# A retention, top-capacity experts and an ELU layer in one kernel: six dense pieces beside the retention, a fetch timed behind its scatters, one ELU step on VectorE

## The chip, the cores and the metric

The kernel runs on one core of a Trainium2 chip. The metric is the device time of one execution in microseconds. The kernel before takes 535.06 us in the median of three runs (534.75 to 536.52). The execution that was profiled took 536.38 us.

## What is computed

Three layers follow each other. All inputs are float32.

```python
# 1: retention over B=2, H=8, S=768, D=64, in blocks of 64, with a state per head
intra = (qb @ kb.T * Dmask) @ vb ; inter = (qb * lam_pow) @ kv_state
out[block] = intra + inter
kv_state = lam_block * kv_state + (kb * rev_pow).T @ vb
# 2: x is [1536, 512]; eight experts, each takes at most 192 tokens
logits = x @ w_gate                       # [1536, 8]
for idx in argsort(-logits.flatten()):    # best pair (token, expert) first
    if token is free and counts[expert] < 192: assign
out[mask_e] = relu(x[mask_e] @ w1[e]) @ w2[e]     # 512 -> 1024 -> 512
# 3: a dense layer over all tokens
h = x @ w_in                              # 512 -> 2048
g = where(h > 0, h, exp(min(h, 0)) - 1)
result = g @ w_out                        # 2048 -> 512
```

The greedy assignment fills one expert after another: the expert whose 192nd token has the highest threshold is closed first, its tokens leave, and the rest is counted again.

## The kernel before

**Retention.** Twelve tiles of 128 tokens (n = 0 to 11) pass through transposes (L292), scores (L316), a masked product (L320 on VectorE), outputs (L329, L340), gate logits (L383, L410) and a state update (L365 on VectorE, L354 on GpSimd). Each tile's best logits are turned into rows (L455, L458) and compared with the others on VectorE (L435, L439, L442, L467). TensorE counts the results in 8-column matmuls (L447), from which a first rank comes.

**The dense pieces.** w_in and w_out arrive as 64-bit numbers in 16 pieces of 1 MB (L224, into the two buffers stg). Each piece is split by five steps: L252, L255 and L258 on VectorE make a float32 f, L260 on ScalarE its float16 high part (wih or woh), and L261 on VectorE the low part (wil or wol). Five pieces are split beside the retention, and the loads of two more are issued there. The other pieces are split beside the experts.

**The experts.** For k = 0 to 7 a choice is made: a threshold (L831, L832, L840), the chosen tokens (L883 to L885), and index counts, 1-column matmuls of `mt` with the shifted one-hot `ohs` (L898), one per tile and per column of `idx`. L904 copies each column. GpSimd then gathers the chosen rows of x from memory (xb at L917, xa at L923). TensorE transposes them (L964), L973 or L976 and L981 copy them as xt, and then come the groups h = x w1 (L1076, or L1043 to L1045 in float16), y = h w2 (L1116, or L1043 to L1045), g = y w_in (L1043 to L1045) and, after each second expert, o = g w_out (L1211 to L1213). h and y pass through ScalarE and VectorE on their way (L1087, L1091, L1126, L1130). The ELU of g (`g_evac`) has three steps on ScalarE (L1183 to L1185), then the maximum on VectorE (L1186), and a split in two float16 halves (L1191, L1192). Outputs leave through ot (L1224) and an indirect store by GpSimd (L1231).

**Updates and packing.** After choice k, `update` takes the remaining tokens' best logits (L763), turns them into rows (transposes L781, copies L784), compares them (L435, L439, L442) and counts (L804). For the choices after k = 1, 3 and 5 the open tokens are first packed: each tile's records are scattered by GpSimd to a packed list in memory (L731) and the list is fetched again (L744, L748). From the third on, each scatter waits for the last TensorE instruction that the program has issued before it.

**What sets the order.** A class `Plan` takes tasks with an engine, a cost, the tasks each depends on, a `lag` after its end and a bonus `ahead`, and places them in time. The order of its `at` times is the order of the instructions on every engine. One plan covers the retention (with the dense pieces beside it), a second one everything from the first threshold on. The numbers there are the author's, not the trace's.

Of the kernel before, what the change touches and what calls it, by code (L numbers as in the profile page):

```python
# [24 lines left out]
OP = mybir.AluOpType  # L25
# [16 lines left out]
LATE = 11  # L42

# [59 lines left out]
def kernel(  # L103
# [82 lines left out]
    def lam_in():  # L186
        nc.scalar.dma_start(lamb, bass.AP(tensor=lam.tensor, offset=lam.offset, ap=[[0, 128], [1, H]]))
# [300 lines left out]
    put("lam", "ACT", 0.5, lam_in, lag=2.8, ahead=100.0)  # L488
    put("dec", "DVE", 2.7, decays, T["eye"], T["lam"], ahead=190.0)
    put("gate", "ACT", 1.9, gate_in, lag=3.0, ahead=90.0)  # L490
    put("qsc", "DVE", 1.6, q_scales, T["lam"], T["dec"], ahead=20.0)
# [10 lines left out]
    for n in range(NT):  # L502
        c = n % NC

        soon = PITCH * (NT - 1 - n) - BEHIND
        if n + 1 < NT:
            fed(n + 1)
# [7 lines left out]
        if c:  # L515
            put(("qS", n), "POOL", 1.3, lambda n=n: q_scaled(n), *of(("qTo", n), ("inter", n - 2), ("inter", n - 3), "qsc"))
# [18 lines left out]
        put(("scored", n), "PE", 0.88, lambda n=n: scored(n), *of("gate", ("xT0", n), ("xT1", n), ("L", n - 2)), mode="A", ahead=soon)  # L535
        put(("L", n), "ACT", 0.18, lambda n=n: logits(n), *of(("scored", n)), ahead=soon)
        put(("m", n), "DVE", 0.18, lambda n=n: top_logit(n), *of(("L", n)), ahead=soon)
        put(("row", n), "PE", 0.22, lambda n=n: row(n), *of(("m", n), ("rowo", n - 1)), mode="A", ahead=soon)
        put(("rowo", n), "ACT", 0.29, lambda n=n: row_out(n), *of(("row", n)), ahead=soon)
# [41 lines left out]
    use, use2 = [None, None], [None, None]  # L581
    for i in range(EARLY_N + NEXT):
        ld = add("SP", 2.9, lambda i=i: load_dense(i), T["ld", "v", 1], use[i % 2])
        if i < EARLY_N:
# [10 lines left out]
            use2[i % 2] = add("DVE", 1.19, lambda go=go: go(4), d)  # L595
# [97 lines left out]
    def pack(k):  # L693
# [45 lines left out]
        for c in range(n):  # L739
# [5 lines left out]
                    p, lag=4.0, ahead=AHEAD)  # L745
# [569 lines left out]
```

## Time and profile before

| | |
|---|---|
| median of three runs | 535.06 us (534.75 to 536.52) |
| the profiled execution | 536.38 us, its span 534.3 us |
| instructions in the span | 12976 |
| TensorE (PE) busy | 507.6 us, 95% of the span |
| VectorE (DVE), ScalarE (ACT), GpSimd (POOL) busy | 360.8, 306.5, 92.9 us |
| mean granted TensorE clock | 0.976 |
| moved by DMA | 70.42 MB, mean 132 GB/s |

The times are microseconds from the start of the span. A matmul's row shows its whole passage, so in a run of matmuls the distance of two starts is what each costs the engine. A DVE or ACT row is an instruction, or, with xN, N of the same kind. What stands in brackets is how long the engine had been idle before that instruction and what released it. In the windows the granted clock is a share of 2.4 GHz.

### The profile page before, as it was taken

What the parts mean: (1) busy time and instruction counts of PE and PEld (TensorE: products, weight loads), DVE (VectorE), ACT (ScalarE), POOL (GpSimd) and SP (SyncE); (2) the same over time, 40 slices, a digit from 0 to 9 for tenths busy, and PEclk for the clock granted to TensorE, in tenths of its full rate; (3) what the DMA queues carried; (4) which work ended last, traced back from release to release, by engine and by line L of the source; (5) the groups of instructions that cost most, each with busy time, mean ns of one, the idle gap of its engine ahead of it and who ended that gap; (6) DMA issues with size and microseconds to landing.
All of it is one profiled execution on the core that took longest, in us unless ns stands there. A gap on an engine that the chain in (4) does not pass through costs nothing.

```text
span 534.3 us, 12976 instructions
## 1 busy us (share of the span) xinstructions
PE 507.6 (95%) x5362; PEld 426.5 (80%) x5362; DVE 360.8 (68%) x808; ACT 306.5 (57%) x646; POOL 92.9 (17%) x124
## 2 busy tenths in 40 slices
PE   8999886899999899999999999999999999999994
PEld 7887776799899874589869956996997489879941
DVE  6689998987999697486587675637557552671510
ACT  5777744324883665445982784468449533961910
POOL 3231420200345002030441101012401001000000
PEclk9999996799999999999999999999999999999997
DMA  9999934394686104240440324052205504040000
GB/s 208 219 285 236 292 127 140 106 372 184 209 299 197 50 1 176 85 144 11 182 162 25 128 80 162 18 190 89 95 3 188 178 21 188 1 178 1 2 21 20
DMA packets 62218, 70.42 MB, mean 132 GB/s; under 512 B 40160, under 2 KB 44720, under 8 KB 61136
## 3 DMA queue, kind: packets, MB, share of 16 engines
q1 hardware_dynamic: 57456, 62.66, 36.6%
q0 software_dynamic: 2960, 6.66, 3.7%
q8 instruction: 42, 0.69, 0.5%
q10 hardware_dynamic: 1744, 0.28, 0.3%
q14 instruction: 16, 0.13, 0.1%
HBM read 63.08 MB, written 6.51 MB: 130 GB/s over the span
## 4 chain that ended last, share of the span: by engine, by line
PE 68%; DVE 15%; issue 6%; DMA 5%; ACT 4%; POOL 1%; POOLq 0%; ACTq 0%; DVEq 0%
PE ps_t L1043 5%; PE ps_t L1044 5%; PE ps_s L1044 5%; PE ps_s L1043 5%; PE ps_s L1045 5%; PE ps_t L1045 5%; PE ps_s L1213 3%; PE ps_s L1211 3%; PE ps_s L1212 3%; PE ps_S L1043 2%; PE ps_S L1044 2%; PE ps_S L1045 2%; PE ps_s L1076 2%; PE ps_t L1211 2%; PE ps_t L1212 2%
## 5 line engine op out<-in xcount | busy, mean ns | idle before, releaser
L1044 PE MATMUL ps_t<-yt,wih 128*128 128x192 f16 x208 | 51.2, 246 | 0.8 <-DVE yt L1130 0.8
L1045 PE MATMUL ps_t<-yt,wil 128*128 128x192 f16 x208 | 51.2, 246 | 0.0
L1043 PE MATMUL ps_t<-yt,wih 128*128 128x192 f16 x208 | 51.1, 246 | 0.0
L1045 PEld LDWEIGHTS <-wil 128*128 128x128 f16 x512 | 50.1, 98 | 1.0 <-issue 0.9
L1043 PEld LDWEIGHTS <-wih 128*128 128x128 f16 x512 | 50.3, 98 | 0.0
L1044 PEld LDWEIGHTS <-wih 128*128 128x128 f16 x512 | 50.0, 98 | 0.2
L1045 PE MATMUL ps_s<-yt,wil 128*128 128x192 f16 x200 | 49.2, 246 | 0.0
L1044 PE MATMUL ps_s<-yt,wih 128*128 128x192 f16 x200 | 49.2, 246 | 0.0
L1043 PE MATMUL ps_s<-yt,wih 128*128 128x192 f16 x200 | 49.2, 246 | 0.0
L731 POOL DMA_INDIRECT open<-rec,dest x27 | 31.3, 1159 | 49.7 <-DVE dest L720 18.3
L1213 PEld LDWEIGHTS <-gg 128*128 128x128 f16 x192 | 18.8, 98 | 23.4 <-DVE gg L1192 0.9
L1213 PE MATMUL ps_s<-woh,gg 128*128 128x512 f16 x96 | 36.4, 379 | 0.4 <-DVE gg L1192 0.4
L1212 PE MATMUL ps_s<-wol,gg 128*128 128x512 f16 x96 | 36.4, 379 | 0.0
L1211 PE MATMUL ps_s<-woh,gg 128*128 128x512 f16 x96 | 36.4, 379 | 0.0
L1192 DVE TENSOR_TENSOR gg<-el,gg 128x384 f16<-128x384 f32 x64 | 34.2, 552 | 1.7 <-ACT gg L1191 1.6
L1035 DVE SCALAR_TENSOR_TENSOR w2p<-stg,w2p 128x1024 f16<-128x1024 f32 x24 | 28.3, 1221 | 10.1 <-ACT w2p L1032 10.1
L1184 ACT ACTIVATE el<-el 128x384 f32<-128x384 f32 x64 | 33.4, 522 | 1.9
L1185 ACT ACTIVATE el<-el 128x384 f32<-128x384 f32 x64 | 33.4, 521 | 1.8
L1212 PEld LDWEIGHTS <-gg 128*128 128x128 f16 x192 | 18.8, 98 | 19.4
L1211 PEld LDWEIGHTS <-gg 128*128 128x128 f16 x192 | 18.8, 98 | 19.2
L1191 ACT ACTIVATE gg<-el 128x384 f16<-128x384 f32 x64 | 31.2, 508 | 2.3 <-DVE el L1186 2.3
L923 POOL DMA_INDIRECT xa<-xd,idx x8 | 9.4, 1175 | 132.4 <-DVE idx L904 131.8
(269 smaller groups left out, 1580.7 us busy)
## 6 DMA issues: line engine op xcount, KB each, us to landing
stg<-in_moe_w_dram SPq DMA_DIRECT2D x24, 1024.0 KB, 5.3
stg<-in_moe_w_in_dram SPq DMA_DIRECT2D x7, 1024.0 KB, 7.2
stg<-in_moe_w_out_dram SPq DMA_DIRECT2D x6, 1024.0 KB, 5.7
w1p<-in_moe_w_dram SPq DMA_DIRECT2D x8, 512.0 KB, 4.3
w2p<-in_moe_w_dram SPq DMA_DIRECT2D x8, 512.0 KB, 8.3
kn<-in_k_dram SPq DMA_DIRECT2D x12, 256.0 KB, 5.5
vn<-in_v_dram SPq DMA_DIRECT2D x12, 256.0 KB, 5.6
xd<-xN SPq DMA_DIRECT2D x12, 256.0 KB, 4.0
```

Source lines behind the costliest of these rows:

```text
L731: st = nc.gpsimd.indirect_dma_start(out=buf, out_offset=bass.IndirectOffsetOnAxis(ap=dest[:, c:c + 1], axis=0), in_=rec[:, c, :], in_offse ...
L1035: nc.vector.scalar_tensor_tensor(part(1), T["t"][:, 1024 * z:1024 * z + 1024], sc, part(0), op0=OP.mult, op1=OP.subtract)
L1043: nc.tensor.matmul(o, wh, xh, start=first, stop=False, skip_group_check=True)
L1044: nc.tensor.matmul(o, wh, xl, start=False, stop=False, skip_group_check=True)
L1045: nc.tensor.matmul(o, wl, xh, start=False, stop=last, skip_group_check=True)
L1184: a = add("ACT", 0.49, lambda: nc.scalar.activation(e_, e_, AF.Exp, scale=-1.0), a, ahead=EAHEAD)
L1185: a = add("ACT", 0.49, lambda: nc.scalar.activation(e_, e_, AF.Copy, scale=SG, bias=-SG), a, ahead=EAHEAD)
L1191: a = add("ACT", 0.49, lambda: nc.scalar.activation(gh, two(e_), AF.Copy), a, *free, ahead=EAHEAD)
L1192: a = add("DVE", 0.53, lambda: nc.vector.tensor_tensor(gl, two(e_), gh, op=OP.subtract), a, ahead=EAHEAD)
L1211: nc.tensor.matmul(p, GH[:, f, c], woh[:, f, :], start=f == 0, stop=False, skip_group_check=True)
L1212: nc.tensor.matmul(p, GH[:, f, c], wol[:, f, :], start=False, stop=False, skip_group_check=True)
L1213: nc.tensor.matmul(p, GL[:, f, c], woh[:, f, :], start=False, stop=f == RF2 - 1, skip_group_check=True)
```

## The change

Ten edits, some of them of numbers that only move the plan.

- `lam` is loaded by GpSimd's queue rather than ScalarE's, and `qsc` is entered later in the plan.
- Six dense pieces rather than five are planned beside the retention. The low step (L261) of the last two of these, pieces 4 and 5, is left to the second plan.
- `HOLD` names a number that was a default, 0.15, and stays at it.
- The fetch of packed tokens is planned 4.3 us behind the last scatter (`(p, 4.3)`), with a lag of its own of 3.0 rather than 4.0.
- On odd k the index counts make two columns rather than three, xb is gathered with 128 rows rather than 64, and the transposed tile is read 64 columns further on (`z0`).
- For k = 0 the second half of the transposed tokens goes to a bank of the ring `work` rather than of `rbank`, where the row transposes take theirs.
- From the third expert on (k = 2 to 7) the third ELU step is a VectorE tensor_scalar rather than a ScalarE copy.

```diff
-EARLY_N, NEXT = 5, 2
-
-LD, PITCH, BEHIND = (1.3, 1.1), 5.5, 2.0
+EARLY_N, NEXT = 6, 2
+
+LEFT_N = 2
+
+LD, PITCH, BEHIND, HOLD = (1.3, 1.1), 5.5, 2.0, 0.15
 AHEAD, XAHEAD, WAHEAD, EAHEAD, GLAG, APART = 15.0, 4.0, 5.0, 3.0, 3.5, 1.2
...
 LATE = 11
+
+LESS_ACT = (2, 3, 4, 5, 6, 7)
...
     def lam_in():
-        nc.scalar.dma_start(lamb, bass.AP(tensor=lam.tensor, offset=lam.offset, ap=[[0, 128], [1, H]]))
+        nc.gpsimd.dma_start(lamb, bass.AP(tensor=lam.tensor, offset=lam.offset, ap=[[0, 128], [1, H]]))
...
     put("orders", "DVE", 0.7, orders, T["eye"], ahead=195.0)
-    put("lam", "ACT", 0.5, lam_in, lag=2.8, ahead=100.0)
+    put("lam", "POOL", 1.0, lam_in, lag=2.8, ahead=100.0)
     put("dec", "DVE", 2.7, decays, T["eye"], T["lam"], ahead=190.0)
     put("gate", "ACT", 1.9, gate_in, lag=3.0, ahead=90.0)
-    put("qsc", "DVE", 1.6, q_scales, T["lam"], T["dec"], ahead=20.0)
...
         if c:
+            if n == 1:
+                put("qsc", "DVE", 1.6, q_scales, T["lam"], T["dec"], ahead=20.0)
             put(("qS", n), "POOL", 1.3, lambda n=n: q_scaled(n), *of(("qTo", n), ("inter", n - 2), ("inter", n - 3), "qsc"))
...
-    use, use2 = [None, None], [None, None]
+    use, use2, left = [None, None], [None, None], []
     for i in range(EARLY_N + NEXT):
...
             d = add("ACT", 1.02, lambda go=go: go(3), d)
-            use2[i % 2] = add("DVE", 1.19, lambda go=go: go(4), d)
+            if i < EARLY_N - LEFT_N:
+                use2[i % 2] = add("DVE", 1.19, lambda go=go: go(4), d)
+            else:
+                left.append((i, go))
     done = hp.order()
...
         fetch = add("POOL", 0.92, lambda: nc.gpsimd.dma_start(new, buf[0:left, :].rearrange("(c p) e -> p c e", p=128)),
-                    p, lag=4.0, ahead=AHEAD)
+                    (p, 4.3), lag=3.0, ahead=AHEAD)
...
-        js = ((0, 128), (64, 0, -64))[k % 2]
+        js = ((0, 128), (64, -64))[k % 2]
+        half = slice(0, 128 if k % 2 else 64)
...
         p = None
-        for j in (1, 0, 2)[0:len(js)]:
+        for j in (1, 0):
             p = add("PE", 0.027 * n, lambda j=j: index(j), (d, 0.3), p, *fills, *(old if j == 1 else ()), ahead=AHEAD)
...
                 nc.vector.tensor_copy(ixm[0:64, k // 2:k // 2 + 1], idx[0:64, k - 1, 1:2])
-                nc.vector.tensor_copy(ixm[64:128, k // 2:k // 2 + 1], idx[64:128, k, 2:3])
-            add("DVE", 0.3, middle, got[2])
+                nc.vector.tensor_copy(ixm[64:128, k // 2:k // 2 + 1], idx[64:128, k, 1:2])
+            add("DVE", 0.3, middle, got[1])
         gb = add("POOL", 1.05, lambda: nc.gpsimd.indirect_dma_start(
-            out=xb[0:64], out_offset=None, in_=xd, in_offset=bass.IndirectOffsetOnAxis(ap=idx[0:64, k, 1:2], axis=0)),
+            out=xb[half], out_offset=None, in_=xd, in_offset=bass.IndirectOffsetOnAxis(ap=idx[half, k, 1:2], axis=0)),
             got[1], *xa_free[0], lag=GLAG, ahead=2 * AHEAD)
...
     def x_parts(k, gb, ga):
-        ca, cb = ((0, 128), (64, 0))[k % 2]
+        ca, cb = ((0, 128), (128, 0))[k % 2]
+        z0 = 64 * (k % 2)
         whole = k in WHOLE
...
             if k == 0:
-                i, old, use = (xbank, rbank)[g].take()
-                tag = ("x", RB_[i])[g]
+                i, old, use = (xbank, work)[g].take()
+                tag = ("x", WB[i])[g]
             else:
...
             def hi(S=S, sl=sl, g=g):
-                pv = S["p"][:, 0:2 * CAP].rearrange("p (a n) -> p a n", a=2)
+                pv = S["p"][:, z0:z0 + 2 * CAP].rearrange("p (a n) -> p a n", a=2)
                 if whole:
...
                 def lo(S=S, sl=sl):
-                    pv = S["p"][:, 0:2 * CAP].rearrange("p (a n) -> p a n", a=2)
+                    pv = S["p"][:, z0:z0 + 2 * CAP].rearrange("p (a n) -> p a n", a=2)
                     nc.vector.scalar_tensor_tensor(xt[:, 1, sl, :], pv, SX, xt[:, 0, sl, :], op0=OP.mult, op1=OP.subtract)
...
         a = add("ACT", 0.49, lambda: nc.scalar.activation(e_, e_, AF.Exp, scale=-1.0), a, ahead=EAHEAD)
-        a = add("ACT", 0.49, lambda: nc.scalar.activation(e_, e_, AF.Copy, scale=SG, bias=-SG), a, ahead=EAHEAD)
+        if k in LESS_ACT:
+            a = add("DVE", 0.3, lambda: nc.vector.tensor_scalar(e_, e_, SG, -SG, op0=OP.mult, op1=OP.add), a, ahead=EAHEAD)
+        else:
+            a = add("ACT", 0.49, lambda: nc.scalar.activation(e_, e_, AF.Copy, scale=SG, bias=-SG), a, ahead=EAHEAD)
         a = add("DVE", 0.53, lambda: nc.vector.tensor_tensor(e_, e_, pv(), op=OP.max), a, ahead=EAHEAD)
...
     R.task = None
+    for i, go in left:
+        dense_done[i] = add("DVE", 1.19, lambda go=go: go(4))
+        f64.uses[i % 2].append(dense_done[i])
     for i in range(EARLY_N, EARLY_N + NEXT):
...
     S_use = work.uses[2]
...
```

TensorE between the first gather and the first expert, before (the tile names: m the best logits, xb and xa the gathered rows, w1p the first weights):

```order
L781 MATMUL ps_o<-identf,m 128x128 x4
L935 MATMUL ps_t_1474<-onesf 128x128 x8
L964 MATMUL ps_x<-identf,xb 128x128 x2
L964 MATMUL ps_m<-identf,xb 128x128 x2
L964 MATMUL ps_x<-identf,xa 128x128 x2
L964 MATMUL ps_m<-identf,xa 128x128 x2
L781 MATMUL ps_m<-identf,m 128x128 x4
L1076 MATMUL ps_s_1615<-xt,w1p 128x192 x8
```

And with the change (gt are the comparisons that L813 counts, L804 before):

```order
L945 MATMUL ps_t_1478<-onesf 128x128 x2
L790 MATMUL ps_o<-identf,m 128x128 x4
L945 MATMUL ps_t_1478<-onesf 128x128
L790 MATMUL ps_m<-identf,m 128x128 x4
L945 MATMUL ps_t_1478<-onesf 128x128 x13
L975 MATMUL ps_x<-identf,xb 128x128 x2
L975 MATMUL ps_s_1608<-identf,xb 128x128 x2
L813 LDWEIGHTS gt_1451
L813 MATMUL ps_o<-oh,gt_1451 128x8
```

The third set of row transposes (L781, now L790) stood behind the gathered rows and stands ahead of them; 12 counting matmuls follow xb, then come xa's transposes, 24 more counts and the first h.

TensorE where the packed tokens of the second packing are turned into rows, before (yt times wih and wil is g of the second expert):

```order
L1045 LDWEIGHTS wil
L1045 MATMUL ps_s_2452<-yt_1444,wil 128x192
L781 MATMUL ps_m<-identf,m 128x128 x4
L781 MATMUL ps_o<-identf,m 128x128 x4
L1043 LDWEIGHTS wih
L1043 MATMUL ps_S<-yt_1444,wih 128x192
L1044 LDWEIGHTS wih
L1044 MATMUL ps_S<-yt_1444,wih 128x192
```

And with the change:

```order
L1056 LDWEIGHTS wil
L1056 MATMUL ps_s_2396<-yt_1448,wil 128x192
L790 MATMUL ps_o<-identf,m 128x128 x4
L790 MATMUL ps_m<-identf,m 128x128 x4
L1054 LDWEIGHTS wih
L1054 MATMUL ps_t_2378<-yt_1448,wih 128x192
L1055 LDWEIGHTS wih
L1055 MATMUL ps_t_2378<-yt_1448,wih 128x192
```

The rows stood behind 72 matmuls of g after the end of y and stand behind 24. The last scatter ahead of them waited for the middle of y's second half and waits now for the last matmul of h.

VectorE at the second half of y of the first expert, before (f_100 and f_99 are pieces being split, idx the index columns, yt the split of y):

```order
L885 TENSOR_TENSOR mt<-me,tid 128x12
L258 SCALAR_TENSOR_TENSOR f_100<-gg,f_100 128x1024
L261 SCALAR_TENSOR_TENSOR wil<-f_99,wih 128x1024
L887 TENSOR_TENSOR act<-act,me 128x12
L700 CAST a_124<-act 128x12
L701 SCALAR_TENSOR_TENSOR a_124<-ones_83,a_124 128x11
L252 TENSOR_SCALAR f_99<-gg 128x1024
L712 COPY rec<-L 128x12x8
L713 CAST rec<-tid 128x12
L255 SCALAR_TENSOR_TENSOR f_99<-gg,f_99 128x1024
L904 CAST idx<-ps_m 128x1 x2
L1130 SCALAR_TENSOR_TENSOR yt_1443<-ps_s_1864,yt_1443 128x384
```

And with the change:

```order
L262 SCALAR_TENSOR_TENSOR f_100<-stg_98,f_100 128x1024
L896 TENSOR_TENSOR act<-act,me 128x12
L709 CAST a_124<-act 128x12
L710 SCALAR_TENSOR_TENSOR a_124<-ones_83,a_124 128x11
L721 COPY rec<-L 128x12x8
L722 CAST rec<-tid 128x12
L727 TENSOR_TENSOR to<-ps_m,after 128x12
L728 TENSOR_TENSOR to<-to,act 128x12
L729 TENSOR_TENSOR dest<-to,after 128x12
L1141 SCALAR_TENSOR_TENSOR yt_1447<-ps_s_1841,yt_1447 128x384
L914 CAST idx<-ps_o 128x1 x2
L1141 SCALAR_TENSOR_TENSOR yt_1447<-ps_t_1883,yt_1447 128x384
```

Of the dense steps ahead of this yt, L261, L252 and L255 have gone behind it. A step L262 (L258 before) of another piece, with its L259 just ahead of the rows shown, stands before the packing's first instructions.

## Rows read from the trace of the kernel before

**Rows 1.** The page, chain that ended last: shares by engine

```profile
PE 68%; DVE 15%; issue 6%; DMA 5%; ACT 4%; POOL 1%; POOLq 0%; ACTq 0%; DVEq 0%
```

**Rows 2.** Windows: PE, PEld, DVE, ACT, POOL busy; clock, DMA share, GB/s

```profile
15.00:30.00 15.00, 14.26 (x208) 11.86 (x208) 11.12 (x19) 11.78 (x40) 4.81 (x5) 1.00 1.01 207
60.00:75.00 15.00, 13.07 (x187) 11.12 (x183) 14.79 (x27) 8.81 (x27) 6.08 (x4) 1.00 0.48 130
75.00:90.00 15.00, 12.20 (x210) 10.69 (x204) 12.97 (x23) 5.40 (x12) 0.00 (x0) 0.73 0.62 211
```

**Rows 3.** PE's waits from 107 us on: us, times, longest

```profile
PE ps_m L781 <- DVE m L763: 2.0, 1, 2.0
PE ps_t L1044 <- DVE yt L1130: 0.8, 1, 0.8
PE ps_m L898 <- ACT ohs L859: 0.4, 1, 0.4
PE ps_s L1213 <- DVE gg L1192: 0.4, 1, 0.4
PE ps_s L1044 <- DVE ht L1091: 0.4, 1, 0.4
```

**Rows 4.** Timeline, 102 to 107 us: start, us, engine, line [idle before]

```profile
103.91 1.22 DVE L261 SCALAR_TENSOR_TENSOR wil<-f,wih 128x1024 f16<-128x1024 f32 x1
104.17 0.44 PE L964 MATMUL ps_x<-identf,xa 128*128 128x128 f32 x2 [1.06 <-DMA xa<-xd,idx]
105.65 1.11 PE L781 MATMUL ps_m<-identf,m 128*128 128x128 f32 x4 [0.82 <-DVE xt L973]
106.56 0.85 PE L1076 MATMUL ps_s<-xt,w1p 128*128 128x192 f32 x2
```

**Rows 5.** Timeline, 133 to 138 us: index counts beside a dense step

```profile
136.03 1.22 DVE L255 SCALAR_TENSOR_TENSOR f<-gg,f 128x1024 uint32<-128x1024 uint32 x1
136.21 0.83 PE L898 MATMUL ps_m<-mt,ohs 128*128 128x1 f16 x27 [0.44 <-ACT ohs L859]
```

**Rows 6.** Timeline, 160 to 182 us: second packing, fetch, row transposes

```profile
162.97 5.36 PE L1116 MATMUL ps_S<-ht,w2p 128*128 128x192 f32 x32
...
171.22 1.34 POOL L731 DMA_INDIRECT open<-rec,dest  x1 [1.35 <-PE ps_t L1116]
177.06 1.06 POOL L744 DMA_DIRECT2D new<-open  x1 [4.50 <-DMA open<-rec,dest]
179.23 0.25 PE L1045 MATMUL ps_s<-yt,wil 128*128 128x192 f16 x1
180.23 0.23 DVE L748 COPY L<-new 128x72 f32<-128x72 f32 x1 [3.71 <-DMA new<-open]
181.47 0.65 PE L781 MATMUL ps_m<-identf,m 128*128 128x128 f32 x4 [2.00 <-DVE m L763]
```

**Rows 7.** Timeline, 226 to 240 us: first and third ot on ACT

```profile
226.35 0.59 ACT L1224 ACTIVATE ot<-ps_S 128x512 f32<-128x512 f32 x1
234.73 0.60 ACT L1224 ACTIVATE ot<-ps_s 128x512 f32<-128x512 f32 x1 [3.87 <-DMA out_dram<-ot,idx]
```

**Rows 8.** Timeline, 0 to 10 us: lam's load and its user

```profile
1.32 0.69 ACTq L187 DMA_DIRECT2D lamb<-in_lam_dram  x1
2.85 0.24 POOL L405 IOTA tid<- 128x12 f16 x1
6.48 2.63 DVE L205 TENSOR_TENSOR_SCAN dec<-lamb,identf 128x128 f32<-128x128 f32 x8 [3.11 <-DMA lamb<-in_lam_dram]
```

**Rows 9.** Timeline, one VectorE step beside a GpSimd step, and alone

```profile
22.85 1.27 POOL L307 TENSOR_TENSOR qS<-qT,qsc 128x512 f32<-128x512 f32 x1 [1.02 <-ACT qT L297]
23.02 1.18 DVE L439 TENSOR_SCALAR w1p<-mrow,m 128x128 f16<-128x128 f32 x1
...
227.81 0.28 DVE L439 TENSOR_SCALAR gt<-mrow,m 128x128 f16<-128x128 f32 x1
```

**Rows 10.** The page, costliest groups: third step of the ELU

```profile
L1185 ACT ACTIVATE el<-el 128x384 f32<-128x384 f32 x64 | 33.4, 521 | 1.8
```

More of the change, by code (lines that the diff above doesn't have):

```diff
@@ L505 @@
         soon = PITCH * (NT - 1 - n) - BEHIND
+        hold = HOLD if n >= NT - 2 else 0.15
         if n + 1 < NT:
@@ L534 @@
                 *of(("intra", n), ("scored", n - 2), ("nat", n - 2), (f"xT{i - 1}", n)))
[L535 to L539, printed above, removed]
+        put(("scored", n), "PE", 0.88, lambda n=n: scored(n), *of("gate", ("xT0", n), ("xT1", n), ("L", n - 2)), mode="A", ahead=soon, look=hold)
+        put(("L", n), "ACT", 0.18, lambda n=n: logits(n), *of(("scored", n)), ahead=soon, look=hold)
+        put(("m", n), "DVE", 0.18, lambda n=n: top_logit(n), *of(("L", n)), ahead=soon, look=hold)
+        put(("row", n), "PE", 0.22, lambda n=n: row(n), *of(("m", n), ("rowo", n - 1)), mode="A", ahead=soon, look=hold)
+        put(("rowo", n), "ACT", 0.29, lambda n=n: row_out(n), *of(("row", n)), ahead=soon, look=hold)
         if n < LATE:
@@ L545 @@
         if n == g1 - 1:
-            put(("best", g0), "DVE", 0.75, lambda c0=g0, c1=g1: best(c0, c1), *of(*[("m", x) for x in range(g0, g1)]), ahead=soon)
+            put(("best", g0), "DVE", 0.75, lambda c0=g0, c1=g1: best(c0, c1), *of(*[("m", x) for x in range(g0, g1)]), ahead=soon, look=hold)
         if n:
             put(("below", n), "DVE", 0.21 + 0.00052 * 128 * n, lambda n=n: below(GT[n][:, 0:n * 128], n, 0, n),
-                *of(("m", n), *[("rowo", x) for x in range(n)]), ahead=soon)
-        put(("tie", n), "DVE", 0.3, lambda n=n: tie(GT[n][:, n * 128:(n + 1) * 128], n), *of(("rowo", n)), ahead=soon)
+                *of(("m", n), *[("rowo", x) for x in range(n)]), ahead=soon, look=hold)
+        put(("tie", n), "DVE", 0.3, lambda n=n: tie(GT[n][:, n * 128:(n + 1) * 128], n), *of(("rowo", n)), ahead=soon, look=hold)
         x = 0
@@ L554 @@
             put(("old", n, x), "DVE", 0.26 * (e - x) if e - x < 3 else 0.2 + 0.00098 * 128 * (e - x),
-                lambda n=n, x=x, e=e: old(n, x, e), *of(("rowo", n)), ahead=soon)
+                lambda n=n, x=x, e=e: old(n, x, e), *of(("rowo", n)), ahead=soon, look=hold)
             x = e
```

## The prediction

> **What bounds the kernel now.** I read first the shares of the chain that ended last: 68% of the span is TensorE (PE), 15% VectorE (DVE), 5% DMA [rows 1]. So the end is the time of the first choice, then TensorE's stream of matmuls, then what TensorE waits inside that stream. The windows show that the retention is another matter: from 60 to 75 us DVE is busy 14.79 of 15 us and PE 13.07, while from 15 to 30 us DVE has 3.88 us free; from 75 us on PE's granted clock is a mean 0.73 of 2.4 GHz, that is, part of the time it stands at 1.2 GHz [rows 2]. The waits of PE from 107 us on are few and each occurs once: 2.0 us for the rows of the packed tokens, 0.8 for a split of y, 0.4 each for the one-hots, a gg and an ht [rows 3]. Four us in all: that is what better order can take back there. Then I read the stretches: the first gather, where PE has three things in a row between 104.17 and 106.56 us [rows 4]; the index counts [rows 5]; the second packing [rows 6].
>
> I sum against the profiled execution, 536.38 us. The median of the runs is 535.06, 1.32 less, and I subtract the same differences from that.
>
> **The change part by part.**
>
> *Fewer index counts.* On the odd k one column of three goes: 12 + 9 + 6 + 3 = 30 matmuls, at 0.83 / 27 = 0.03 us [rows 5]: -0.9 us. PE is the bound there, so all of it counts. xb's gather moves 128 rows for 64, and xa already moves 128 in its own gather, so I cost it at nothing: the two are issued one after the other and the later one ends last in either case.
>
> *The first gather.* Before, xa's transposes start at 104.17 and end at 104.83 (105.65 less the 0.82 of idle); PE then waits for the copy of xt, because the row transposes L781 want the bank that is being copied, does these in 1.11 us, and starts h at 106.56: 2.39 us after xa came [rows 4]. In the new order the row transposes stand ahead of the gathered rows, inside the wait for the gather, and 36 of the 144 counts of the first update do too: 12 before xa's transposes and 24 behind them. This stretch runs at about half the clock: the same four transposes take 1.11 us at 105.65 and 0.65 at 181.47 [rows 4, 6]. So 24 counts are 24 x 0.06 = 1.5 us, so h starts at 104.83 + 1.5 = 106.3; the copies of xt are done by then, even with some of DVE's comparisons ahead of them (0.4 us). That is -0.3, and the 36 counts are gone from the full-speed stream behind, 36 x 0.03 = -1.1. Sum -1.4. The ends: -2.2 if the 24 counts cost nothing (1.11 + 1.1); +0.2 if a dense step of 1.22 us [rows 4] comes in front of xt's copy on DVE.
>
> *The second half of y.* PE lost 0.8 us because the split yt stood on DVE behind a dense step L255 of 1.22 us that began at 136.03, and 0.44 because the counts waited for ohs [rows 3, 5]. In the new order L261, L252 and L255 have gone behind yt. I take -1.2. Queued ahead of yt stand now the three instructions of dest, which themselves wait for the packing's counts: if these are late, yt is late; the other end is +1.2, one dense step's worth.
>
> *The packing.* The last scatter starts at 171.22, after half of the second half of y: each half of y takes 5.2 us (5.36 less what overlaps), the first from 162.97, so the second from 168.17 to 173.37 and its middle at 170.8. From that mark to the rows at 181.47 are 10.7 us: scatter, its landing, fetch at 177.06, copy at 180.23, rows [rows 6]. PE has work until 179.31, 72 matmuls of g from 173.37, 0.0825 each, and then idles 2.0. In the new order the mark is the end of h, before y: 10.4 us of y and 24 matmuls of g (2.0) lie between mark and rows, 12.4 us against 10.7 wanted. With 1.7 us to spare the wait goes: -2.0. What is late next is the counts behind, which wait for DVE's comparisons. The ends are -2.0 and, if the scatters ahead are slower than their marks, 0. The packings for k = 4 and 6 had no wait and have 11.9 and 10.9 us by the same count of the new order's matmuls.
>
> *Third ELU step.* 48 ScalarE steps of 0.52 us [rows 10], 25 us, go; DVE gets 48 of its own. The trace has no such step: a DVE step of 128 columns took 0.28 us [rows 9], one of 1024 took 1.22 [rows 4], and 384 columns lie between; I take 0.45. Both engines have time in these experts, so only the 0.4 that PE waits for a gg [rows 3] comes back: -0.4. The ends are -0.4 and +0.8, should the 0.45 stand in front of a split that PE waits for.
>
> *The outputs beside the third expert.* Here the new order of ScalarE is worse. The third ot waits for the first store to land: 3.87 us of idle, from ot at 226.35 to ot at 234.73 [rows 7]. Before, two high steps of the second weights stood ahead of it; now it stands ahead of them and of the first splits of h. They cost 1 us each and y needs the first of them at once. Below, nothing, if the earlier first ot moves the store as much; above, 3.87. I take +1.0, one high step.
>
> *The retention.* Three DVE steps of the sixth piece come in, at most 3 x 1.22 = 3.7 us, and a low step of piece 4 (1.22) goes out: +2.4 at most on DVE, and one ScalarE step and 1 MB of load more. The new order pulls the second piece's load right behind the first, and so its steps into the stretch where DVE has 3.88 us free [rows 2]. I take +0.3. If DVE's free time there can't be had, +2.4; if the two low steps that leave the tail were on the chain, -2.4. What a step costs beside GpSimd shows at 23.02: L439 on 128 columns took 1.18 us while qS ran on GpSimd, and 0.28 alone [rows 9]. Three new steps can each meet that, 3 x 0.9 = +2.7 more as the upper end.
>
> The Trainium skill, "SBUF — State Buffer", section "Who interferes with whom", says that VectorE and GpSimd share a port pair that one instruction holds whole, so that the other stands still until it is done. The row at 23.02 agrees. By that rule the sixth piece costs a third of 2.7, 0.9 us, since GpSimd is busy about a third of the retention, and the sum below would be 0.6 higher.
>
> *lam.* ScalarE's issue at 1.32 landed at 6.48, and DVE waited 3.11 for it. GpSimd is free at 3.09 [rows 8]. Its queue needs from 3.2 us (the fetch, 177.06 to 180.23) [rows 6] to the 5.2 that ScalarE's load took [rows 8], so lam lands between 6.3 and 8.3: -0.2 to +1.8. I take +0.3, nearer to the row of the same queue. That DVE, and PE behind it, wait at 6 us is not all lost: I count it whole.
>
> *qsc later, HOLD.* qsc's user is far behind it, and HOLD keeps its value: nothing.
>
> Sum: -0.9 - 1.4 - 1.2 - 2.0 - 0.4 + 1.0 + 0.3 + 0.3 = -4.3 us. That makes 532.1 for an execution like the profiled one and 530.8 for the median.
>
> **The rivals.**
>
> *The sixth piece lies on the retention's chain.* For it: DVE is full from 60 us on [rows 2]. Against it: the early stretch is not. Then the first choice is later by 2.4 + 1.8 (lam) + 0.9 (one step beside GpSimd) = 5.1 in place of 0.6, and the end is 530.8 + 4.5 = 535.3: no change.
>
> *The clock falls earlier: the slower side.* PE is at full clock from 15 to 75 us, and falls after its first gaps in the 75 to 90 window [rows 2]. Place: 60 to 75 us, where PE is busy 13.07. If DVE's extra steps open gaps there and PE is put at 1.2 GHz, its 13.07 us become 26.1, and the window is 11 us longer: 530.8 + 11 = 542. [...] Against it: the piece's steps sit early.
>
> *The third ot takes the place of the fetch.* The packing's wait goes, but all 3.87 us of ScalarE's wait fall on y of the third expert: 530.8 + 2.9 = 533.7, or a little less than no change. The same time follows if the change doesn't do what it says and the rows at the second packing still wait for 2 us, with +1 for ot.
>
> *More comes back.* The two low steps shorten the tail by 2.4, ot costs nothing, the piece and lam cost nothing: 530.8 - 2.4 - 1.0 - 0.6 = 526.8.
>
> **How the numbers follow.** The forecast, from 528.5 to 533.4, has a chance of 0.5; more comes back 0.14; the third ot or the old wait 0.14; the sixth piece on the chain 0.13; the clock 0.09. A run of this kernel tells 0.3%, 1.6 us, from no change: faster is below 533.5, slower above 536.7. Faster gets 0.5, 0.14 and half of the ot case: 0.71. Same gets the other half and two thirds of the sixth piece: 0.15. Slower gets the clock and the rest: 0.14. The range runs from 525.5, below the case of more, to 537, past the sixth piece.
>
> **What would show it.** In the new profile: no idle PE ahead of the row transposes of the second packing; the row transposes of the first update before xa's; yt of the first expert's second half ahead of L261; xa's transposes within 1 us of 104.17 [rows 4]; DVE idle for lam between 2.9 and 4.9; a PE wait of about 1 us in y of the third expert. The prediction is wrong if the gathered rows come 3 us later, if the granted clock falls before 75 us, or if PE's few waits come back elsewhere in the same sum.

## The result, and the profile after

The changed kernel takes 529.55 us in the median of 15 runs (527.98 to 534.74), the kernel before in the same sittings 536.18 (15 runs, 532.69 to 538.88). The ratio is 0.9888, with a 95% interval of 0.9866 to 0.9910: faster by 1.1%, 6.0 us. The prediction was 530.8. The profiled execution of the changed kernel took 527.98 us, its span 526.0; it is the fastest of the 15, so I lean on differences of stretches rather than on the 8.4 us between the two profiled executions.

One cut serves all runs below: the matmul behind the first threshold (L840 before, L849 after), ahead of which lies the retention and behind which the stream of the experts. In the timelines of the kernel before and of the changed kernel it is:

```profile
93.80 0.61 PE L840 MATMUL ps_o<-th,onesf 128*128 128x16 f32 x2 [2.32 <-DVE th L832]
```

```profile
93.87 0.61 PE L849 MATMUL ps_o<-th,onesf 128*128 128x16 f32 x2 [1.97 <-DVE th L841]
```

From there to the end of the span are 440.5 us before and 432.1 after. Between these two profiles the 8.3 us of span come from behind the cut, and none from ahead of it.

The chain that ended last, by engine, on the page of the changed kernel:

```profile
PE 78%; DVE 15%; issue 3%; DMA 1%; POOL 1%; POOLq 0%; ACT 0%; DVEq 0%
```

TensorE went from 68% to 78%, DMA from 5% to 1% [rows 1]. The windows (columns as in [rows 2]):

```profile
15.00:30.00 15.00, 13.66 (x194) 11.91 (x194) 10.46 (x18) 11.98 (x44) 4.77 (x4) 1.00 1.03 243
60.00:75.00 15.00, 14.11 (x185) 11.92 (x186) 13.80 (x29) 9.70 (x33) 5.39 (x6) 1.00 0.61 189
105.00:120.00 15.00, 15.00 (x208) 14.54 (x205) 14.71 (x31) 2.26 (x5) 0.00 (x0) 1.00 1.01 368
```

From 60 to 75 us TensorE gained 1.04 us of busy time and DVE lost 1.0, so the sixth piece did not fill that window [rows 2]; nor the one from 15 to 30, where DVE is busy 10.46 us for 11.12. From 105 to 120 us TensorE is busy all the time at full clock. What TensorE waited for from 104 us to the end is one line:

```profile
PE ps_t L1087 <- DVE el L1200: 0.6, 1, 0.6
```

The five waits of the kernel before [rows 3], 4 us, are gone; this one is new. The first gather, on TensorE:

```profile
100.65 0.88 PE L790 MATMUL ps_m<-identf,m 128*128 128x128 f32 x4
101.37 3.07 PE L945 MATMUL ps_t<-onesf 128*128 128x128 f32 x26
104.27 0.38 PE L975 MATMUL ps_x<-identf,xb 128*128 128x128 f32 x2
104.71 0.45 PE L813 MATMUL ps_o<-oh,gt 128*128 128x8 f16 x12
105.01 0.42 PE L975 MATMUL ps_x<-identf,xa 128*128 128x128 f32 x2
105.48 0.74 PE L813 MATMUL ps_o<-oh,gt 128*128 128x8 f16 x24
106.09 1.22 PE L1087 MATMUL ps_t<-xt,w1p 128*128 128x192 f32 x6
```

The third row transposes (100.65) stand ahead of the gathered rows, 12 counts behind xb and 24 behind xa, and h starts 1.08 us after xa's transposes, where it was 2.39 [rows 4]. But xa's transposes come 11.1 us after the cut and not 10.4. xa's load was issued at 99.75 us and landed 3.7 us later, near 103.4, and no idle time stands ahead of the transposes: 26 filler matmuls (L945, ones times ones, whose result nothing uses) run until 104.3, then xb's transposes and 12 counts. So xa's rows wait for filler. The second y of the first expert on DVE, and the second packing:

```profile
131.56 0.55 DVE L1141 SCALAR_TENSOR_TENSOR yt<-ps_t,yt 128x384 f16<-128x384 f32 x1
132.03 1.21 DVE L265 SCALAR_TENSOR_TENSOR wil<-f,wih 128x1024 f16<-128x1024 f32 x1
```

```profile
159.65 1.11 POOL L740 DMA_INDIRECT open<-rec,dest  x1 [1.54 <-PE ps_S L1087]
162.18 1.07 POOL L753 DMA_DIRECT2D new<-open  x1 [1.42 <-DMA open<-rec,dest]
171.59 0.60 PE L790 MATMUL ps_o<-identf,m 128*128 128x128 f32 x4
```

The split yt stands ahead of L265 and no wait follows [rows 5]. The last scatter came 11.9 us ahead of the rows and the fetch was issued 2.5 us behind the scatter, where it had been 5.8 [rows 6]; TensorE runs straight into the rows. The outputs beside the third expert, on ScalarE, and the first matmul of its y:

```profile
217.39 0.59 ACT L1238 ACTIVATE ot<-ps_t 128x512 f32<-128x512 f32 x1
224.06 0.60 ACT L1238 ACTIVATE ot<-ps_t 128x512 f32<-128x512 f32 x1 [3.53 <-DMA out_dram<-ot,idx]
224.55 2.00 ACT L1043 ACTIVATE w2p<-stg 128x1024 f16<-128x1024 f32 x2
228.50 2.00 ACT L1043 ACTIVATE w2p<-stg 128x1024 f16<-128x1024 f32 x2 [1.19 <-DMA stg<-in_moe_w_dram]
```

```profile
230.81 0.24 PE L1054 MATMUL ps_t<-ht,w2p 128*128 128x192 f16 x1
```

In the kernel before, that first matmul of y was:

```profile
237.62 0.24 PE L1043 MATMUL ps_s<-ht,w2p 128*128 128x192 f16 x1
```

The third ot still waits 3.53 us for a store [rows 7], but all of this sits earlier: 6.8 us ahead of that y, where it stood 2.9 ahead. Last, lam, and tile 0's output matmuls behind it:

```profile
2.93 0.73 POOL L191 DMA_DIRECT2D lamb<-in_lam_dram  x1
8.46 1.69 DVE L209 TENSOR_TENSOR_SCAN dec<-lamb,identf 128x128 f32<-128x128 f32 x5 [5.08 <-DMA lamb<-in_lam_dram]
13.37 0.43 PE L344 MATMUL ps_o<-wol,vn 128*64 128x128 f32 x2 [1.51 <-DVE wol L324]
```

lam came 2.0 us later than before [rows 8] and TensorE idled 1.51 us for it. The page's line of the new ELU step:

```profile
L1197 DVE TENSOR_SCALAR el<-el 128x384 f32<-128x384 f32 x48 | 17.3, 361 | 15.6 <-ACT el L1195 15.6
```

It costs 0.36 us, between the 0.28 and 1.22 of the prediction's two rows.

### The profile page after: what moved, and what is told of

Same layout as the page of the kernel before. It is cut to its first block, busy times and chain, and to the rows that moved or that the text cites. A ratio compares the mean times of both kernels' runs of the same rounds, so it can differ in the third digit from the quotient of the medians.

```text
span 526.0 us, 12906 instructions
## 1 busy us (share of the span) xinstructions
PE 503.7 (96%) x5332; PEld 423.5 (81%) x5332; DVE 375.5 (71%) x852; ACT 286.8 (55%) x598; POOL 95.2 (18%) x125
## 3 DMA queue, kind: packets, MB, share of 16 engines
HBM read 63.61 MB, written 6.51 MB: 133 GB/s over the span
## 4 chain that ended last, share of the span: by engine, by line
PE 78%; DVE 15%; issue 3%; DMA 1%; POOL 1%; POOLq 0%; ACT 0%; DVEq 0%
PE ps_t L1054 5%; PE ps_s L1054 5%; PE ps_t L1055 5%; PE ps_s L1055 5%; PE ps_t L1056 5%; PE ps_s L1056 5%; PE ps_S L1054 3%; PE ps_S L1056 3%; PE ps_S L1055 3%; PE ps_t L1225 3%; PE ps_s L1225 3%; PE ps_s L1227 3%; PE ps_t L1226 3%; PE ps_s L1226 3%; PE ps_t L1227 3%
## 5 line engine op out<-in xcount | busy, mean ns | idle before, releaser
L1056 PE MATMUL ps_s<-yt,wil 128*128 128x192 f16 x208 | 51.2, 246 | 0.0
L1055 PE MATMUL ps_s<-yt,wih 128*128 128x192 f16 x208 | 51.1, 246 | 0.0
L1054 PE MATMUL ps_s<-yt,wih 128*128 128x192 f16 x208 | 51.1, 246 | 0.0
L740 POOL DMA_INDIRECT open<-rec,dest x27 | 34.4, 1274 | 91.0 <-DVE dest L729 65.6
L1205 ACT ACTIVATE gg<-el 128x384 f16<-128x384 f32 x64 | 32.3, 513 | 8.9 <-DVE el L1200 8.4
L1195 ACT ACTIVATE el<-el 128x384 f32<-128x384 f32 x64 | 33.4, 522 | 1.8
L1046 DVE SCALAR_TENSOR_TENSOR w1p<-stg,w1p 128x1024 f16<-128x1024 f32 x24 | 28.3, 1220 | 7.5 <-ACT w1p L1043 7.5
L1227 PE MATMUL ps_t<-woh,gg 128*128 128x512 f16 x80 | 30.3, 379 | 0.0
L1226 PE MATMUL ps_t<-wol,gg 128*128 128x512 f16 x80 | 30.3, 379 | 0.0
L1225 PE MATMUL ps_t<-woh,gg 128*128 128x512 f16 x80 | 30.3, 379 | 0.0
L1197 DVE TENSOR_SCALAR el<-el 128x384 f32<-128x384 f32 x48 | 17.3, 361 | 15.6 <-ACT el L1195 15.6
```

Of the source, the lines that this page charges most:

```text
L740: st = nc.gpsimd.indirect_dma_start(out=buf, out_offset=bass.IndirectOffsetOnAxis(ap=dest[:, c:c + 1], axis=0), in_=rec[:, c, :], in_offse ...
L1046: nc.vector.scalar_tensor_tensor(part(1), T["t"][:, 1024 * z:1024 * z + 1024], sc, part(0), op0=OP.mult, op1=OP.subtract)
L1054: nc.tensor.matmul(o, wh, xh, start=first, stop=False, skip_group_check=True)
L1055: nc.tensor.matmul(o, wh, xl, start=False, stop=False, skip_group_check=True)
L1056: nc.tensor.matmul(o, wl, xh, start=False, stop=last, skip_group_check=True)
L1195: a = add("ACT", 0.49, lambda: nc.scalar.activation(e_, e_, AF.Exp, scale=-1.0), a, ahead=EAHEAD)
```

## The experiments

The ratios are against the kernel before in the same sitting. Its median was between 535.98 and 536.76 us in four sittings (the changed kernel; e1 to e4; e5 to e8; e9 and e10), so runs of different sittings are compared by their ratios. The cut and the stretch behind it are from each run's one profile. Most runs are planned anew, so an edit can move instructions far from its own place.

| run | median us | ratio, 95% interval | cut at | cut to end |
|---|---|---|---|---|
| before | 536.18 | 1 | 93.8 | 440.5 |
| changed | 529.55 | 0.9888, 0.9866 to 0.9910 | 93.9 | 432.1 |
| e1, lam alone moved, ahead of q | 530.05 | 0.9886, 0.9854 to 0.9917 | 96.3 | 431.8 |
| e2, old bank | 531.47 | 0.9934, 0.9890 to 0.9979 | 95.7 | 433.7 |
| e3, old fetch | 533.21 | 0.9928, 0.9905 to 0.9952 | 95.7 | 435.6 |
| e4, ELU on ScalarE | 531.38 | 0.9930, 0.9888 to 0.9972 | 94.1 | 433.9 |
| e5, lam behind q | 527.79 | 0.9839, 0.9814 to 0.9864 | 95.0 | 432.1 |
| e6, e5 with five pieces | 527.80 | 0.9856, 0.9828 to 0.9884 | 92.8 | 432.9 |
| e7, e5 with none left | 530.11 | 0.9897, 0.9871 to 0.9923 | 95.4 | 432.6 |
| e8, before with the new bank | 533.44 | 0.9959, 0.9937 to 0.9981 | 94.2 | 436.3 |
| e9, before with the new fetch | 534.27 | 0.9965, 0.9933 to 0.9997 | 93.0 | 437.3 |
| e10, e5 with three columns | 529.44 | 0.9881, 0.9829 to 0.9934 | 92.3 | 434.5 |
| e11, before again (one execution) | 534.81 | | 93.5 | 439.2 |
| e12, changed again (one execution) | 529.41 | | 95.6 | 432.1 |

**The two kernels once more (e11, e12).** Nothing is edited.

> The kernel before, profiled once more. Its first profile showed TensorE at 1.2 GHz from 105.7 to 109.1 us, behind 1.06 and 0.82 us of idle, which cost h 1.3 us; the kernel before with the new fetch has the same idle times there and full clock. Theory: the fall is an accident of that execution and not of the order: the granted clock from 105 to 120 us is 0.97 or more, and from the threshold's matmul to the end are 439.0 us or less (440.5 in the first profile). Rival: it belongs to the order, and both come again.

> The changed kernel, profiled once more. Its profiled execution was the fastest of 15 (527.98, median 529.55). Theory: from the threshold's matmul to the end it always takes 432.1 us (within 0.4), and what differs between executions lies ahead of that matmul: 93.9 to 95.7, by the clock that is granted while tile 0 waits for lam. Rival: the executions differ behind it, and the stretch to the end is 1 us or more longer in this one.

e11's window from 105 to 120 us and its wait for xt's copy:

```profile
105.00:120.00 15.00, 14.50 (x169) 14.12 (x170) 13.96 (x30) 3.52 (x7) 0.00 (x0) 1.00 0.99 366
```

```profile
PE ps_m L781 <- DVE xt L973: 0.8, 1, 0.8
```

```profile
105.50 0.65 PE L781 MATMUL ps_m<-identf,m 128*128 128x128 f32 x4 [0.82 <-DVE xt L973]
```

The wait came again, the fall of the clock did not (the four row transposes behind it took 0.65 us, and 1.11 in the first profile [rows 4]): 439.2 us to the end, near the 439.0 expected. So 1.3 us of the 440.5 were an accident of one execution, and the change is worth 7.1 us behind the cut. e12's stretch behind the cut is 432.1 again, and its cut comes 1.8 us later, with this ahead of it:

```profile
10.00:20.00 10.00, 8.32 (x82) 6.79 (x84) 5.67 (x16) 6.71 (x23) 2.63 (x3) 0.83 1.08 308
```

As expected, the changed kernel's executions differ ahead of the cut: in e12 the clock is a mean 0.83 from 10 to 20 us (1.00 in the first profile); it falls at 14 us, just behind tile 0's wait for lam. Of the five profiles with this retention (the changed kernel twice, e2, e3, e4), three show that fall and have the cut at 95.6 or 95.7; two do not and have it at 93.9 and 94.1.

**lam (e1, e5).** e1 changes one word, e5 issues the same load behind q's:

```diff
     def lam_in():
-        nc.gpsimd.dma_start(lamb, ...)
+        nc.scalar.dma_start(lamb, ...)       # e1; in e5 this line is lam_behind, and lam_in is empty
...
         eng.dma_start(t, ...)                # load(n, z)
+        if eng is nc.scalar:                 # e5: q of tile 0, then lam
+            lam_behind()
```

> The changed kernel with lam's load issued by ScalarE's queue again, and not one other instruction moved. In the changed kernel lam came at 8.46 us, 2.0 later than before (6.48), and yet the first threshold's matmul came at 93.87 (93.80 before). Theory: the two us lie on the retention's chain and the rest of the change made them good; then lam comes at 6.5, the threshold's matmul near 91.9, and the time is 2.0 us less (about 527.5). Rival: the retention is paced by its loads, which have the same 1 MB more to carry, so the start is absorbed: threshold within 0.4 us of 93.9 and the same time.

ScalarE's queue and TensorE in e1:

```profile
0.77 0.46 ACTq L191 DMA_DIRECT2D lamb<-in_lam_dram  x1
1.27 0.60 ACTq L156 DMA_DIRECT2D qn<-in_q_dram  x1
```

```profile
7.82 1.09 PE L296 MATMUL ps_t<-identf,qn 128*128 128x128 f32 x4 [2.76 <-DMA qn<-in_q_dram]
```

lam landed at 4.72 us, but ahead of q in that queue, and TensorE then waited 2.76 us for q. Behind that wait the clock was low too:

```profile
10.00:15.00 5.00, 4.55 (x42) 4.00 (x44) 1.29 (x2) 3.44 (x12) 0.71 (x1) 0.55 1.18 308
```

The cut came at 96.3, 2.4 us later than in the changed kernel's first profile and 0.7 later than in e12; the ratio is the changed kernel's (0.9886 and 0.9888). The theory fell. Of the rival, the same time came, and the cut within 0.4 us of 93.9 did not. The run moved two things and was of use only to show which.

> The changed kernel with lam's load on ScalarE's queue, this time behind the first tile's q (in the run with lam alone moved it stood ahead of q, and q came 2.3 us later). No other instruction moves. In the changed kernel tile 0's output matmuls (L344) start at 13.37 us after 1.51 us of idle TensorE, and 11.39 before. Theory: lam's lateness runs through the whole retention; lam lands near 6.5, L344 of tile 0 starts near 11.4, the threshold's matmul comes near 91.9 in place of 93.87, and the time is 2 to 3 us less than the changed kernel's (526.5 to 527.5), since the slow clock that two profiles showed at 14 to 18 us after that idle time goes too. Rival: the loads or VectorE's later steps pace the retention and the threshold stays within 0.5 us of 93.9: same time.

DVE and TensorE in e5, and two windows of it:

```profile
6.51 2.63 DVE L214 TENSOR_TENSOR_SCAN dec<-lamb,identf 128x128 f32<-128x128 f32 x8 [3.13 <-DMA lamb<-in_lam_dram]
11.42 0.43 PE L349 MATMUL ps_o<-wol,vn 128*64 128x128 f32 x2
```

```profile
35.00:40.00 5.00, 4.90 (x51) 3.93 (x51) 4.26 (x10) 1.05 (x3) 2.83 (x2) 0.76 0.95 309
55.00:60.00 5.00, 5.00 (x54) 4.00 (x54) 4.80 (x7) 3.17 (x6) 1.45 (x2) 0.70 1.05 294
```

lam came at 6.51 and tile 0 at 11.42, 2.0 sooner, as expected. The median is 1.8 us below the changed kernel's, 2.6 by the ratios, and the intervals of the two ratios just fail to overlap (0.9864 and 0.9866): the theory's 2 to 3 us hold in time. In this profile the cut still came at 95.0, which looked like the rival, but the windows show why: the granted clock is 0.76 and 0.70 in stretches where e10, with the same order of instructions up to the cut, has full clock and its cut at 92.3:

```profile
35.00:40.00 5.00, 5.00 (x67) 4.20 (x67) 4.47 (x11) 2.18 (x6) 2.71 (x2) 1.00 0.97 301
55.00:60.00 5.00, 4.53 (x63) 3.94 (x58) 3.94 (x8) 3.74 (x10) 0.65 (x1) 1.00 1.07 357
```

So lam behind q is worth 1.5 us or so ahead of the cut (93.9 less 92.3, one profile each, without such a fall), and this version beats both kernels. None of the four profiles with lam behind q (e5, e6, e7, e10) shows the fall at 14 us.

**The pieces (e6, e7).**

```diff
-EARLY_N, NEXT = 6, 2
+EARLY_N, NEXT = 5, 2     # e6, with LEFT_N = 0
-LEFT_N = 2
+LEFT_N = 0               # e7, with EARLY_N = 6
```

> The kernel with lam behind q, with five pieces beside the retention and none of their low steps left over, as before the change (planned anew, so its retention is the one of the kernel before). Theory: the sixth piece with two low steps left over shortens the retention by about 2 us, which is why lam's 2 us did not show; then the threshold's matmul comes at 93.8 as before, 2 us later than with six pieces. Rival: the order of the pieces is worth nothing there, and the threshold comes at the same time as with six pieces (within 0.5 us).

> The kernel with lam behind q and six pieces, but with all six low steps inside the retention (planned anew). It tells which half of that edit matters. Theory: leaving two low steps over is what shortens the retention's tail; without it the threshold comes 2 to 2.5 us later (two steps of 1.14). Rival: the early placing of the second piece is what does it: the threshold moves by less than 0.7 us.

e6 has the same median as e5 (527.80 and 527.79); its cut, 92.8 without a fall of the clock, is 0.5 later than e10's, at the bound that the rival set. The rival holds for the pair of edits: the sixth piece with two low steps left over is worth nothing that can be measured. e7, six pieces with no step left over, is 2.3 us slower than e5, as its theory says, and than e6 (the ratio intervals of e6 and e7 overlap a little). So by the medians the sixth piece alone costs time, and the two low steps left over give it back. But e7's profile has a fall of the clock of its own from 50 to 60 us, so how much of its later cut is the low steps' stays open.

**The bank (e2, e8).** e2 takes the edit out of the changed kernel, e8 puts it alone into the kernel before:

```diff
-                i, old, use = (xbank, work)[g].take()
-                tag = ("x", WB[i])[g]
+                i, old, use = (xbank, rbank)[g].take()
+                tag = ("x", RB_[i])[g]
```

> The changed kernel with the second half of the first transposed tokens in the bank ring of the row transposes again (planned anew with that). Theory: the third row transposes stand behind xt's copy again, PE idles 0.8 to 1.2 us at 105, the clock falls to 1.2 GHz behind that idle time and h's first eight matmuls cost twice: 2.5 to 3.5 us more. Rival: the clock that rose at 101 us stays, as the fall in the kernel before had to do with what was ahead of the gather: 1 us more. Second rival: the row transposes find a place by other edits and nothing is lost.

> The kernel before with one edit: the second half of the first transposed tokens in the ring work (planned anew). Theory: this alone gives the row transposes their place ahead of the gathered rows; the idle 0.8 us and the slow clock at 105 to 109 us go, and h starts about 0.5 us sooner: 2 to 3.5 us less than the kernel before. Rival: the clock's fall at 105 us does not hang on that wait, and only about 1.5 us come back (the wait and the 36 counts). Second rival: without the other edits the plan finds no better order and the time is the same.

Waits and a window of e2:

```profile
PE ps_m L790 <- DVE xt L984: 0.7, 1, 0.7
PE ps_m L908 <- ACT ohs L868: 0.6, 1, 0.6
PE ps_t L1055 <- DVE yt L1141: 0.3, 1, 0.3
```

```profile
105.00:120.00 15.00, 14.29 (x153) 13.74 (x152) 14.52 (x31) 3.50 (x6) 0.00 (x0) 1.00 0.92 326
```

The wait for xt's copy is back, the clock stays at 1.00, and the stretch behind the cut is 1.6 us longer: the first rival, about 1 us, with waits at the counts and the split of the first expert's second y beside it (136 and 138 us). e8 gained 2.2 us by its ratio and 2.9 behind the cut against e11, within its theory's bounds; but part of the theory, the clock, is out, since e11 has full clock without the edit. Nor is all of the 2.9 the first gather's. In e8 the planner also cleared the second y's waits (1.2 us in e11), the wait at the second packing fell from 2.0, and one for a w1p is new:

```profile
PE ps_o L781 <- DVE m L763: 1.3, 1, 1.3
PE ps_s L1045 <- DVE w1p L1035: 0.7, 1, 0.7
```

The second y's waits went with this edit in e8 and came back in part without it in e2.

**The fetch (e3, e9).**

```diff
-                    (p, 4.3), lag=3.0, ahead=AHEAD)
+                    p, lag=4.0, ahead=AHEAD)
```

> The changed kernel with the fetch's old numbers in the plan (a lag of 4.0 and nothing behind the last scatter; planned anew with that). Theory: the rows of the second packing are placed too early again and PE idles about 2 us ahead of them: 2 us more. Rival: the scatters come earlier by the other edits (the packing's instructions are ahead of the dense steps), so the wait stays away: no change.

> The kernel before with the fetch's new numbers in the plan alone (planned anew with that). Its last scatter waits for a matmul 1.5 us later in the stream than the changed kernel's, and its rows stand 11.4 us of matmuls behind that (10.7 wanted before, and 9.2 in the kernel before). Theory: the 2.0 us of idle TensorE ahead of the rows of the second packing go and nothing else moves: 1.5 to 2.2 us less than the kernel before. Rival: the new order pays with the same kind of wait at the next counts or split of y, as the changed kernel with the old fetch showed at 243 to 247 us (1.5 us): less than 0.7 us gained.

The cut is e3's; e9 is the reverse of it in the kernel before. e9 kept its other waits and got a new one for an xt:

```profile
PE ps_m L781 <- DVE xt L973: 0.9, 1, 0.9
PE ps_t L1044 <- DVE yt L1130: 0.7, 1, 0.7
PE ps_x L964 <- ACT xt L973: 0.6, 1, 0.6
```

The 2.0 at the rows is gone; from the cut to the end it is 1.9 us shorter than e11, and the ratio says 1.9 (0.2 to 3.6 by its interval): its theory. e3 fits its rival where that speaks of the second packing, since no wait came back there. e3 lost elsewhere, at the fourth expert's choice and the third expert's yt (245 and 246 us):

```profile
PE ps_m L908 <- ACT ohs L868: 0.5, 1, 0.5
PE ps_S L1055 <- DVE yt L1141: 0.3, 1, 0.3
```

Behind these the granted clock falls, and with that the stretch is 3.5 us longer:

```profile
245.00:250.00 5.00, 4.56 (x41) 4.22 (x42) 1.96 (x8) 1.75 (x5) 3.90 (x5) 0.66 0.93 326
```

TensorE stands at half clock for 3.4 us of that, which makes about 1.7 us of the 3.5. By the ratios e3 lost 2.1 us against the changed kernel. So the fetch's numbers take the wait at the packing away in the kernel before. In the changed kernel the earlier scatters do that without them, and the loss in e3 is not shown to be theirs: e10 has the new numbers and like waits at the same choice (0.5 and 0.2 us).

**The ELU step (e4).**

```diff
-LESS_ACT = (2, 3, 4, 5, 6, 7)
+LESS_ACT = ()
```

> The changed kernel with the third ELU step on ScalarE in all experts again (planned anew with that). Theory: ScalarE's 25 us more bring back the waits of PE at ht and gg beside the third and fourth experts: 0.5 to 1.5 us more. Rival: these waits went by the new order alone: no change, less than 0.3 us of idle PE after 107 us beyond that of the changed kernel. Second rival: with ScalarE crowded the third ot's wait for its store reaches y of the third expert: 2 us or more.

```profile
PE ps_t L1227 <- DVE gg L1206: 1.0, 1, 1.0
PE ps_t L1055 <- DVE ht L1102: 0.2, 1, 0.2
```

Two waits, for a gg (267 us) and an ht (233 us), came back and the stretch behind the cut is 1.8 us longer: the theory, a little above its bounds. The third ot did not reach y.

**The index columns (e10).** The edit of the index columns is taken back, with z0 at 0 and xb of 64 rows:

```diff
-        js = ((0, 128), (64, -64))[k % 2]
-        half = slice(0, 128 if k % 2 else 64)
+        js = ((0, 128), (64, 0, -64))[k % 2]
+        half = slice(0, 64)
...
-        for j in (1, 0):
+        for j in (1, 0, 2)[0:len(js)]:
...
-        ca, cb = ((0, 128), (128, 0))[k % 2]
+        ca, cb = ((0, 128), (64, 0))[k % 2]
```

> The kernel with lam behind q, with three index columns on the odd experts again and xb of 64 rows (planned anew). Theory: 30 one-column matmuls come back at 0.03 us each on an engine without gaps: 0.8 to 0.9 us more, near 528.6, and 30 more matmuls in the trace. Rival: they fall into waits of TensorE, and nothing is seen in the time or in TensorE's waits.

Behind the cut it is 2.4 us longer than e5, 1.65 in the median and 2.3 by the ratios. Its trace has 150 index counts for 120. At 0.03 us the 30 matmuls make 0.8 to 0.9; the rest is waits of the re-planned order, where e5 has one of 0.5 for an el alone:

```profile
PE ps_t L1092 <- DVE el L1205: 1.0, 1, 1.0
PE ps_m L913 <- ACT ohs L873: 0.5, 1, 0.5
```

The theory holds and its price is too low by what the order adds.

**What the four add up to.** Taken back one at a time, the bank, the fetch, the ELU step and the index columns lengthen the stretch behind the cut by 1.6, 3.5, 1.8 and 2.4 us, 9.3 together. That is more than the 7.1 that the whole change gives, since each time the planner writes another order with waits of its own. So these numbers are not shares of the 7.1.

## Why the prediction was right, point by point

- **Fewer counts**, -0.9: the 30 matmuls are gone from the trace and come back in e10. That they make 0.8 to 0.9 of its 1.65 to 2.4 us is worked out from their price and not measured alone.
- **The first gather**, -1.4: h starts 12.2 us after the cut and 12.4 in e11, -0.2, and the 36 counts are out of the stream behind, 1.0 to 1.1. The 24 counts cost 0.61 us from start to start (105.48 to 106.09), not 1.5. I had priced them at the half clock that I read at 105.65, and that fall belonged to one execution: e11 does not have it, and the changed kernel is at full clock there. What I had not seen is that filler matmuls then hold xa's transposes back by 0.7.
- **The second half of y**, -1.2: both waits are gone. The order that clears them came with the bank's edit (e8, e2); they also stay away in e6 and e7, where no low step is left over.
- **The packing**, -2.0: gone, and e9 shows it alone. In the changed kernel it stays gone with the old numbers (e3), so there the early mark of the scatter does it, as I had argued, though I had asked for 10.7 us to the rows and there 8.7 from the scatter are enough. The margin was larger than I made it: the fetch went out 2.5 us behind the scatter and not 5.8.
- **Third ELU step**, -0.4: e4 says -1.8. The step itself is cheaper (0.36 us for 0.45); what I missed is that in the new order ScalarE's 25 us would have cost more waits than the one seen before.
- **The outputs beside the third expert**, +1.0: this wait did not come. The third ot does stand ahead of the high steps and waits 3.53 us, but I had set aside the end that I named myself, that an earlier first ot moves the store as much. The first ot moved 2 us ahead of y (13.4 us for 11.3), and the third followed it after 6.7 us for 8.4, so the high steps were done by 230.5 and y began without a wait. The ht wait of 0.4 went too. That is 1.4 us between forecast and result.
- **The retention**, +0.3: by the cuts of e10 and e6, one profile each, -0.5, and nothing by the medians of e5 and e6. That hides two parts: e7 is 2.3 us slower than both by the median, so the piece's own cost and what the two low steps give back, the two ends that I had named (+2.4 and -2.4), nearly cancel; how much of the 2.3 is the clock's is open. DVE's stalls beside GpSimd are no more than before: eight steps in the changed kernel and nine before take over 0.4 us longer than short steps of their operation and form, 7.1 us in all in either. Each of these rows overlaps a GpSimd tensor_tensor, which agrees with the Trainium skill's rule ("SBUF — State Buffer", "Who interferes with whom"). But the 0.9 us that I drew from it did not come.
- **lam**, +0.3: mis-sized. It landed 2.0 us later, just above the upper end of 1.8. I took the fetch's 3.2 us because it is the same queue; at the start of the program, with all loads under way, this load took 5.5 from its issue, near ScalarE's 5.2. And it runs through the retention: without a fall of the clock the cut comes at 92.3 with lam behind q and at 93.9 in the changed kernel, 1.5 us where I had put 0.3.
- A wait that I did not name, 0.6 us for an el at 151 us.

Sum behind the cut: forecast -4.9, measured -7.1 (e11 to e12), and -8.3 against the profile that I summed from, with its accident. The traces account for the 7.1. From the start of one matmul to the next, e11's seven waits behind h take 5.6 us and the changed kernel's one 0.7; each is some 0.15 more than the idle time in its bracket, which I had left out of every wait that I priced. The 66 counts fewer make 1.7 to 2.0 at 0.025 to 0.03 each, and h comes 0.2 sooner: 6.8 to 7.1.

Ahead of the cut: forecast +0.6, measured 0 to +2. The two errors have opposite signs, which brought the total within 1.3 us, and in part that is luck: the fall itself was 6.0 us for a forecast of 4.3, and the kernel before stood 1.1 us higher in these sittings than in the three runs that I subtracted from.

The rival of the sixth piece is out for the change as it stands (e6). So is that of the clock as I put it: it needed DVE's steps to open gaps from 60 to 75 us, and TensorE was busier there. Yet the clock did fall ahead of 75 us in e12, which I had named as a sign of being wrong. It does not count against the change, since e11, the kernel before, has such a fall too (0.70 from 40 to 45 us). Where the same order ran with and without falls, their price was 1.8 us for the one of e12 and 2.7 us for the two of e5.

## What to carry to other kernels

Split the span at a matmul through which everything passes, and compare the two parts by themselves: here the part behind it repeated to 0.1 us in two executions of the changed kernel while the part ahead moved by 1.8. Look at the clock in both parts all the same: in the kernel before, one fall behind the cut made 1.3 us. An order that a planner writes is judged by the waits that are left, not by the edit: the fetch's numbers removed a wait at the packing in the kernel before, and taking them out of the changed kernel brought none back there and two at 245 us. And a small load at the start of a program, on which the first tile depends, is worth its place in a queue: here behind the one load that was needed sooner, and ahead of the others.

## What the runs showed of the hardware that was not expected

- The granted clock fell in some executions and not in others of the same order, ahead of the cut: 0.83 from 10 to 20 us in e12 and 1.00 in the first profile of the changed kernel; 0.76 and 0.70 in two 5 us stretches of e5 and 1.00 in e10. In the first profile of the kernel before it fell at 105 us behind idle times of 1.06 and 0.82 us; e2 (0.71), e9 (0.34 and 0.86) and e11 (0.42 and 0.82) had like ones there and kept 1.00 from 105 to 120 us.
- A 4 KB load ahead of a 256 KB load in one queue made the second land 2.3 us later (q at 7.69 us in e1, 5.38 in the kernel before), with 0.50 us between the issues.
- The new tensor_scalar of 128x384 float32 on VectorE took 0.36 us, the same step on ScalarE 0.52 [rows 10].
